# Three-product scores for three batches, 48-row paced loads, and warming products only at the start, in a recurrence-plus-attention kernel

## The chip, the cores and the metric

One core of a Trainium2 chip runs the whole program in one launch. The metric is device time in microseconds (us) of one execution; lower is better. Engines are named as in the profile: PE (TensorE products), PEld (its weight loads), DVE (VectorE), ACT (ScalarE), POOL (GpSimd), SP (the engine that issues the DMAs here).

## What is computed

A gated linear recurrence over 768 steps (4 batches, 8 heads of 48 channels), then four causal attention experts over its output, of which each row takes its best two. In the input, wq and wk are scaled by about 29, so that the scores are large.

```python
for t in range(S):                                  # S = 768, D = 48
    cur = np.einsum('bhd,bhe->bhde', u[None] * kt, vt)
    y[:, :, t] = np.einsum('bhd,bhde->bhe', rt, state + cur)
    state = wt[:, :, :, None] * state + np.einsum('bhd,bhe->bhde', kt, vt)
...
for e in range(E):                                  # E = 4, D = 384, Hd = 64
    q = x @ wq[e]; k = x @ wk[e]; v = x @ wv[e]
    scores = scale * (q @ k.transpose(0, 2, 1))
    scores = np.where(causal, -1000000000.0, scores)
    a = np.exp(scores - scores.max(-1, keepdims=True))
    a /= a.sum(-1, keepdims=True) + 1e-09
    ye = a @ v @ wo[e]
    # added to the rows whose best two experts include e, times the gate
```

## The kernel before, in words

The work is cut into eight units, one for each batch b and half g of the sequence (384 rows). A unit has two parts. The recurrence (`rwkv`, from line 316 on) works on four pairs of heads p: SP loads the streams of decay, key and receptance (tile `lt`, 128 partitions of 1166 numbers, each head padded from 48 to 64 partitions), the same data in row order (`nat`) and the values (`vy`). DVE and POOL form decay products and running products (`w2`, `suf`, `pre`, `kt`, with `kw` and `rw` written in place into `lt`), PE transposes the keys (`ktp`), forms state updates (`ups`), in-chunk scores (`aps`) and outputs (`yps`), DVE carries the state from chunk to chunk (`wst`, line 406). The attention (`moe`, from line 623 on) works for two pairs of experts ep: projections `proj` (line 665; product of high and low parts, three products each in the format fp32r for every unit but the first), evacuation of Q and K from PSUM (`qd`, lines 674 to 680), values (`vproj`), scores (`sc`, line 761), maximum on DVE (line 771), exponential on ACT (line 776), transposes of the weights (`tp`), product with the values (`av`, line 818) and the output projection (`op`, line 886).

A score tile takes 128 rows of Q against 128 to 768 columns of K, with the two experts of a pair in the upper and lower 64 rows of PE's array. Q and K are float32 there:

```python
for h in range(np_):
    o = slice(h * w, (h + 1) * w)
    for x in range(2):
        p = slice(64 * x, 64 * x + 64)
        nc.tensor.matmul(spv(x)[:, h, :], q()[p, t], flat(k())[p, o], start=True, stop=True)
```

PE transposes 128x128 blocks in one of two ways (`turn`, lines 217 to 224): whole (line 220) where the product ahead of it uses the whole array, and as two 64-row halves side by side (line 224) where the array is already split.

The order of all instructions is written out by hand in the string `ORDER` (line 975 on): a letter for the engine and the number of the planned operation. `Plan.order` (line 125) walks through it, gives out buffers and emits. Each engine executes its own instructions in that order; across engines only data, buffers and semaphores bind. SP's loads wait only for their buffer (four `lt`, three `nat`, three `vy`) and for a free DMA semaphore. `warm` (line 938) are products on zeros with no reader; 33 of the 94 planned stand in the order, all in the early part.

Of the kernel before, what the change touches and what calls it, by code (L numbers as in the profile page):

```python
# [27 lines left out]
WB = NH * (C2 + 1) + 1  # L28

# [6 lines left out]
def t_scan(cols):  # L36
    return 95 + 2.09 * cols
# [10 lines left out]
def t_pool(cols):  # L48
    return {144: 415, 192: 550, 199: 580, 240: 655, 288: 785, 384: 905}[cols]
# [142 lines left out]
def rwkv_moe(ctx: ExitStack, tc: tile.TileContext, wkr, vY, nat, uN, uT,  # L192
# [9 lines left out]
    def sb(shape, dt, tag, name):  # L202
        return Slot(wk, shape, dt, tag, name)

# [111 lines left out]
    def rwkv(b, g, v0, v1):  # L316
# [54 lines left out]
        def keys(group, n):  # L371
# [25 lines left out]
            for x, (p, kt, kts, vn, na, suf, sfv, ys) in enumerate(group):  # L397
                want(p / (NP + 1))
                ws, kw = wst[p], ("wst", p)
                for c in range(NH - g):  # L400
                    i, a = divmod(c, 2)

                    def grow(e, c=c, o=columns(x, a, i), ws=ws, sfv=sfv):
                        new = ws[0:112, c0 + c, :]
                        if c0 + c:
                            nc.vector.scalar_tensor_tensor(new, ws[0:112, c0 + c - 1, :], sfv()[0:112, c, 0:1], upk()[0:112, o], op0=ALU.mult, op1=ALU.add)  # L406
                        else:
                            copy(e, new, upk()[0:112, o])
                    if c0 + c:
                        plan.add("ws", {"DVE": 172}, grow, [upk, suf, kw + (c0 + c - 1,)], [kw + (c0 + c,)])  # L410
                    else:
                        plan.add("us", {"ACT": 200, "DVE": 115}, grow, [upk], [kw + (0,)])
# [5 lines left out]
                plan.add("ys", {"DVE": t_dve((NH - 1 + g) * D), "POOL": t_pool((NH - 1 + g) * D)}, scaled, [suf] + [kw + (c0 - g + c,) for c in range(NH - 1 + g)], [ys])  # L418
# [3 lines left out]
        for p in range(NP):  # L422
            n = f"{b}{g}{p}"
            want(p / (NP + 1))
            lt = sb([128, 2 * WB + 2 * NH * C], F32, "lt", f"lt{n}")
            if first and p == 0:
                load("ld", lambda lt=lt: lt()[:, 0:2 * WB], wkr[b, g, p, :, 0:2 * WB], 2 * WB, [(lt, 0)])
                load("ld", lambda lt=lt: lt()[:, 2 * WB:], wkr[b, g, p, :, 2 * WB:], 2 * NH * C, [(lt, 1)])
            else:
                load("ld", lt, wkr[b, g, p], 2 * WB + 2 * NH * C, [(lt, 0), (lt, 1)])  # L430
# [53 lines left out]
            if first:  # L484
# [13 lines left out]
                plan.add("rkm", {"PE": 360}, sums, [(na, 1), "ut"], [rkb], mode="Q")  # L498
# [5 lines left out]
                plan.add("rk", {"DVE": 145, "ACT": 390}, kept, [rkb], [rk])  # L504
# [22 lines left out]
            if not first:  # L527
# [12 lines left out]
                plan.add("rk", {"DVE": t_dve(288), "ACT": 1250}, rks, [(na, 2)], [rk, (na, 2)])  # L540
# [9 lines left out]
            plan.add("ux", dict(prod(288), ACT=1370), ux, [vy if first else (na, 0), rk], [(xn, p)])  # L550
# [72 lines left out]
    def moe(b, g, v0, v1):  # L623
# [7 lines left out]
        if g == 0:  # L631
            BT["K"] = [sb([128, 2, 384], F32, f"K{ep}", f"K{b}{ep}") for ep in range(2)]
            BT["v"] = [sb([128, NT, 128], F32, f"v_sb{ep}", f"v_sb{b}{ep}") for ep in range(2)]
        K, v_sb = BT["K"], BT["v"]
        Q = [sb([128, 384], F32, f"Q{ep}", f"Q{n0}{ep}") for ep in range(2)]
# [11 lines left out]
        def proj(ep, qk):  # L647
# [4 lines left out]
            for k in range(3):  # L652
# [10 lines left out]
                def mm(e, k=k):  # L663
                    for j, (w, x) in enumerate(((wqh, xh), (wql, xh), (wqh, xl))):
# [3 lines left out]
                         claim=[(K if qk else Q)[ep]])  # L668
            if qk == 0:
# [35 lines left out]
        def gates():  # L705
# [15 lines left out]
            plan.add("gate", {"DVE": 365}, compare, lgk, [m1, c1, c2])  # L721
# [7 lines left out]
            plan.add("gate", {"POOL": 1440}, ranks, lgk + ["masks", m1], [c1, c2, rank, ge])  # L729
            plan.add("gate", {"ACT": 250}, lambda e: nc.scalar.activation(ge(), ge(), AF.Exp), [ge], [ge])  # L730
# [7 lines left out]
            plan.add("gate", {"POOL": 875}, norm, [ge, c1], [gs, c1])  # L738

        def scores(ep, i):  # L740
# [8 lines left out]
            q, k = Q[ep], K[ep]  # L749

# [11 lines left out]
            plan.add("sc", {"PE": T_SC[3 * g + i]}, mm, [q] + [(k, gg) for gg in range(g + 1)],  # L762
# [63 lines left out]
        def gather(i0, i1):  # L826
# [12 lines left out]
            plan.add("g3", {"DVE": 610}, over, [(asum, i, x) for i in range(i0, i1) for x in range(E)] + [ge, gs], [gg])  # L839
# [91 lines left out]
    plan.add("masks2", {"DVE": 1400}, masks2, [], ["masks"])  # L931
# [19 lines left out]
    held = None  # L951
    for o in plan.order(dict(PE=7200.0 - 216 * WARM[0], DVE=3000.0, ACT=1700.0, POOL=3000.0, SP=1800.0)):
# [5 lines left out]
        e = o["e"]  # L958
        if e in BOTH and o["kind"] in BOTH[e]:
# [13 lines left out]
BUFS.update(K0=2, K1=2, Q0=2, Q1=2)  # L973
# [3 lines left out]
P29 P30 P31 P32 P33 P126 V139 A127 V143 P34 P140 S113 P128 V146 A141 V144 V147 P15 S171 S138 A129 V148 P8 P11 S235 V145 P151 V176 A152 P18 V149 P10  # L977
P153 V177 P161 P25 S236 S196 V173 A125 S172 V198 S250 V130 G180 V178 V131 P6 V162 G205 A154 P12 P28 V132 V164 G182 S4 V133 P35 P174 V155 V134 G135
V179 P185 A175 P14 V201 A186 V206 A150 V202 S99 P187 P166 V238 V188 V156 G207 V189 V157 A0 V190 V158 V191 G181 A167 V159 V192 A184 S197 P36 P210 V203
V193 G160 P199 V183 V204 G194 S289 P168 V239 A211 A200 V208 P212 V246 A169 S251 V242 A213 P37 P229 V253 P220 V214 A230 G243 V240 V215 A209 V216 S104  # L980
V247 V241 V217 S304 G245 V221 A248 V223 P1127 P1131 G219 V244 P225 A249 V257 S107 V254 V258 P227 V259 S252 A226 V255 V218 A100 S290 V261 V296 P231
A228 V292 P265 V256 A232 P233 S291 V293 P1128 A234 S352 A266 V307 V260 P1129 A267 V294 V297 P268 V101 A1130 A105 P281 S305 V308 V262 P1074 V300 A263
A264 P1075 S367 V295 P1076 V301 P1066 V312 V299 P1067 V106 S237 V298 A1077 P1070 P1071 A284 A1078 V311 S408 V360 P1072 V313 V275 G315 V282 A1073 A302
V276 P1132 P1068 S368 V309 V269 G285 V277 V270 P319 V1079 V271 V278 V272 G359 P1086 V279 A320 V273 P1087 V310 G280 A321 P1133 V370 V355 G274 V314 P322
V356 S423 P335 A1069 A303 V371 P286 V329 A338 G375 G316 V330 V323 V324 V331 G378 A1134 V325 V332 P1088 A102 V326 S306 V357 V287 P19 S353 V333 A317 P26
V327 G374 P1080 V288 P1081 V103 G334 P1097 A318 P1106 G328 V415 V358 P1082 V1107 G339 V1109 A1108 V1098 V336 P1115 A1084 A1090 A1110 G361 V1100 P1111
V1091 V1085 V372 P340 A1112 V373 A1101 A1099 V1116 G416 V1118 A1117 G377 P1104 V341 P1113 A1105 V342 A1114 P1120 V376 A1119 P1102 P346 V362 S488 A1103
A1121 V411 P1122 A347 V1092 P400 A1123 V412 A1083 A1089 V348 P349 G379 S409 V403 A350 P343 P1124 G430 A344 A380 S369 S473 G1093 V401 P1125 P1126 V345
# [149 lines left out]
```

## Time and profile before

| | us |
|---|---|
| device time, median of 3 runs | 338.61 |
| lowest and highest run | 336.25, 338.82 |
| profiled execution, span from first to last instruction | 335.0 |
| PE busy, DVE busy, ACT busy, POOL busy | 315.5, 267.8, 237.6, 142.2 |
| DMA: bytes moved, mean rate | 44.13 MB, 132 GB/s |

For the profiled execution only the span is given, no device time of its own; the median of the runs is 3.6 us above that span and the lowest run 1.3 us. The busy times add up what each engine executes, with PE's ends modelled. A chain of waits is followed back from the last instruction; "issue" in it is time in which an engine waited for nothing that the profile shows.

### The profile page before, as it was taken

To read this page: it belongs to the slowest core of one execution; us is meant where nothing else is said; L and a number is where in the kernel's file an instruction comes from. 1 tells how busy PE (TensorE), PEld (TensorE's weight loads), DVE (VectorE), ACT (ScalarE), POOL (GpSimd) and SP (SyncE) were. 2 spreads that over 40 slices of the span, in tenths; PEclk is the share of its full clock that TensorE was granted. 3 is DMA by queue.
4 is the path that set the end of the run, shared out by engine and by line. 5 is a ranking of instruction groups with operands and counts; after the bars stand their busy time and mean duration, and the time that the engine had idled before them with its cause. 6 is when DMAs were issued, how large, how long until landed. Compare 5 with 4: busy or idle time off the path is not lost.

```text
span 335.0 us, 12951 instructions
## 1 busy us (share of the span) xinstructions
PE 315.5 (94%) x5174; PEld 246.3 (74%) x5174; DVE 267.8 (80%) x863; ACT 237.6 (71%) x842; POOL 142.2 (42%) x275
## 2 busy tenths in 40 slices
PE   8969988999999997969999999999999999999995
PEld 3647666777866975869777758789778867877684
DVE  6978989999999897957979887999765565675752
ACT  2358888998899774936787968758856484548861
POOL 2341166478565567532666646573600000310230
PEclk9998999999999999998999999999999999999999
DMA  7997760654625486372563092532000001001021
GB/s 259 323 285 269 235 214 34 232 179 129 223 102 215 143 268 210 97 251 72 157 202 108 4 346 73 155 90 70 4 0 26 0 3 48 3 25 70 2 72 70
DMA packets 18204, 44.13 MB, mean 132 GB/s; under 512 B 2144, under 2 KB 10080, under 8 KB 18144
## 3 DMA queue, kind: packets, MB, share of 16 engines
q1 hardware_dynamic: 18144, 43.30, 38.7%
q8 instruction: 41, 0.67, 0.8%
q14 instruction: 19, 0.16, 0.1%
HBM read 38.58 MB, written 4.72 MB: 129 GB/s over the span
## 4 chain that ended last, share of the span: by engine, by line
PE 82%; DVE 10%; issue 5%; ACT 2%; POOL 0%; POOLq 0%
PE pp L665 13%; PE yp L818 12%; PE sp L761 10%; PE op L886 7%; PE vp L697 6%; PE tp L224 4%; PE aps L572 4%; PE tp L220 4%; PE yps L350 3%; PE ups L395 3%; PE yps L348 3%; PE pp L658 2%; PE warm L938 2%; DVE wst L406 2%; DVE a L771 2%
## 5 line engine op out<-in xcount | busy, mean ns | idle before, releaser
L776 ACT ACTIVATE a<-a,mx 128x256 f32<-128x256 f32 (+5 forms) x96 | 64.2, 670 | 10.2 <-DVE mx L771 8.6
L771 DVE CUSTOM_DVE_ANT_0 a<-sp,causal 128x384 f32<-128x384 f32 (+5 forms) x96 | 56.4, 616 | 15.0 <-PE sp L761 8.8
L228 ACT COPY ATa<-tp 128x512 f32<-128x512 f32 (+3 forms) x73 | 35.2, 490 | 24.1 <-PE tp L224 12.2
L761 PE MATMUL sp<-K,Q 64*128 64x384 f32 (+4 forms) x256 | 45.9, 470 | 0.5 <-DVE mx L771 0.4
L406 DVE SCALAR_TENSOR_TENSOR wst<-wst,suf,ups 112x48 f32<-112x48 f32 x160 | 35.9, 256 | 3.8 <-ACT wst L228 2.9
L818 PE MATMUL yp<-ATa,v_sb 128*64 128x384 f32 (+2 forms) x240 | 36.3, 430 | 0.2 <-DVE ge L731 0.2
L546 ACT ACTIVATE xn<-nat,rk 128x48 f32<-128x48 f32 x132 | 32.2, 331 | 0.7 <-DVE rk L539 0.7
L665 PE MATMUL pp<-xh,wh_qk 128*128 128x384 f32 x84 | 31.6, 376 | 0.0
L350 PE MATMUL yps<-ys,pre 64*64 64x48 f32 (+1 forms) x704 | 25.4, 220 | 6.4 <-issue 6.4
L761 PEld LDWEIGHTS sp<-K,Q 64*128 64x128 f32 x256 | 21.6, 187 | 10.7 <-issue 4.5
L350 PEld LDWEIGHTS yps<-ys,pre 64*64 64x64 f32 (+1 forms) x704 | 22.3, 134 | 9.1 <-issue 8.3
L665 PE MATMUL pp<-xh,wl_qk 128*128 128x384 f32 x84 | 29.0, 345 | 0.0
L665 PE MATMUL pp<-xl,wh_qk 128*128 128x384 f32 x84 | 28.9, 344 | 0.0
L224 PEld LDWEIGHTS tp<-ident,a 64*128 64x128 f32 x442 | 19.2, 138 | 12.9 <-ACT ATa L228 4.0
L416 POOL TENSOR_TENSOR ys<-wst,suf 112x240 f32<-112x240 f32 (+1 forms) x32 | 25.4, 805 | 4.1 <-DVE wst L406 2.3
L348 PE MATMUL yps<-vy,am 64*64 64x48 f32 x768 | 25.9, 220 | 0.4 <-issue 0.4
L818 PEld LDWEIGHTS yp<-ATa,v_sb 128*64 128x64 f32 x240 | 15.3, 136 | 14.5 <-issue 9.2
L224 PE MATMUL tp<-ident,a 64*128 64x64 f32 x442 | 23.1, 228 | 2.1 <-issue 1.3
L348 PEld LDWEIGHTS yps<-vy,am 64*64 64x64 f32 x768 | 23.1, 134 | 0.0
L697 PE MATMUL vp<-wh_vg,xh 128*128 128x260 f32 x63 | 19.7, 313 | 2.6 <-issue 2.6
L537 ACT ACTIVATE nat<-nat 128x48 f32<-128x48 f32 x90 | 20.6, 236 | 0.9 <-ACT ATa L228 0.5
L518 POOL TENSOR_TENSOR kt<-lt,suf 128x384 f32<-128x384 f32 x19 | 17.8, 936 | 6.5 <-DVE suf L507 1.9
(152 smaller groups left out, 859.7 us busy)
## 6 DMA issues: line engine op xcount, KB each, us to landing
lt<-in_wkr_dram SPq DMA_DIRECT2D x31, 583.0 KB, 5.3
nat<-in_nat_dram SPq DMA_DIRECT2D x28, 432.0 KB, 4.0
vy<-in_vY_dram SPq DMA_DIRECT2D x32, 144.0 KB, 3.8
out_dram<-ob SPq DMA_DIRECT2D x24, 192.0 KB, 2.0
w_qk<-in_wqk_dram SPq DMA_DIRECT2D x1, 768.0 KB, 6.9
nat<-in_nat_dram SPq DMA_DIRECT2D x4, 144.0 KB, 5.9
w_vg<-in_wvg_dram SPq DMA_DIRECT2D x1, 390.0 KB, 6.6
lt<-in_wkr_dram SPq DMA_DIRECT2D x1, 384.0 KB, 3.2
```

Source lines behind the costliest of these rows:

```text
L224: nc.tensor.transpose(o()[:, h * 512 + i * 64:h * 512 + i * 64 + 64], src[r], ident[r, r])
L228: nc.scalar.copy(o, i)
L348: nc.tensor.matmul(to, am()[k, c, :], vy()[k, c, :], start=zero and x == 0, stop=not first and i == 2 and x == len(group) - 1)
L350: nc.tensor.matmul(to, pre()[r, c, 0:C], ys()[r, c, :], start=i == x == 0, stop=False)
L406: nc.vector.scalar_tensor_tensor(new, ws[0:112, c0 + c - 1, :], sfv()[0:112, c, 0:1], upk()[0:112, o], op0=ALU.mult, op1=ALU.add)
L546: nc.scalar.mul(xn()[:, i, (2 * p + h) * D:(2 * p + h + 1) * D], v()[:, i, h, :], rk()[:, i, h:h + 1])
L665: nc.tensor.matmul(pp()[:, 0:384], w[:, qk, k, cs], x()[:, k, :], start=(k == j == 0), stop=(k == j == 2))
L697: nc.tensor.matmul(vp()[:, 0:260], x()[:, k, o], w[:, k, :], start=(k == j == 0), stop=(k == j == 2))
L761: nc.tensor.matmul(spv(x)[:, h, :], q()[p, t], flat(k())[p, o], start=True, stop=True)
L771: nc.vector.tensor_tensor_reduce(out=a()[:, 0:n].rearrange("p (a n) -> p a n", a=np_), in0=spv(x), in1=causal[:, S - n:S].rearrange("p (a ...
L776: plan.add("exp", {"ACT": t_exp(n)}, lambda e, x=x, y=y, mx=mx, a=a: nc.scalar.activation(a()[:, 0:n], a()[:, 0:n], AF.Exp, bias=mx(), sca ...
L818: nc.tensor.matmul(yp()[e * 64:e * 64 + 64, lo:hi], v_sb[ep]()[:, j, e * 64:e * 64 + 64], at, start=(j == 0), stop=(j == nj - 1))
```

## The change

For batches 1, 2 and 3 (`SPLIT`) Q and K are stored in fp32r (the high part), and a second tile each (`Ql`, `Kl`) takes what is left of the projection in PSUM after the high part is subtracted (kind `ql`, DVE). A score is then three fp32r products that add up in PSUM: Q with K, Ql with K, Q with Kl. Batch 0 keeps its float32 scores. The loads of `lt` for all units but the first are two DMAs of 48 rows each into four kept tiles whose padding rows stay from the first unit's loads. Every SP instruction waits in addition for the last PE instruction that stands ahead of it in the order ("pace"). Of the warming products 14 are left instead of 33. The order is written anew as a whole, with it the split of some operations between DVE, ACT and POOL, and some costs in the plan. The scratch space for DMA descriptors is set to 2048 bytes.

```diff
-            lt = sb([128, 2 * WB + 2 * NH * C], F32, "lt", f"lt{n}")
+            lt = streams(f"lt{n}")
...
+                def rows(e, lt=lt, p=p):
+                    for h in range(2):
+                        nc.sync.dma_start(lt()[64 * h:64 * h + D, :], wkr[2 * b + g - 1, p, h])
+                plan.add("ld", {"SP": 1300}, rows, w=[(lt, 0), (lt, 1)])
...
+                if b in SPLIT:
+                    plan.add("ql", {"DVE": t_dve(384)}, lambda e: nc.vector.scalar_tensor_tensor(
+                        Ql[ep](), pp()[:, 0:384], 0.125, h().bitcast(F32), op0=ALU.mult, op1=ALU.subtract), [pk, h], [Ql[ep]])
...
+                if b in SPLIT:
+                    plan.add("ql", {"DVE": t_dve(384)}, lambda e: nc.vector.tensor_tensor(
+                        Kl[ep]()[:, g, :], pp()[:, 0:384], h()[:, g, :].bitcast(F32), op=ALU.subtract), [pk, (h, g)], [(Kl[ep], g)])
...
+            terms = [(q, k), (Ql[ep], k), (q, Kl[ep])] if split else [(q, k)]
...
-                    for x in range(2):
-                        p = slice(64 * x, 64 * x + 64)
-                        nc.tensor.matmul(spv(x)[:, h, :], q()[p, t], flat(k())[p, o], start=True, stop=True)
+                    for j, (q_, k_) in enumerate(terms):
+                        for x in range(2):
+                            p = slice(64 * x, 64 * x + 64)
+                            nc.tensor.matmul(spv(x)[:, h, :], q_()[p, t], flat(k_())[p, o], start=j == 0, stop=j == len(terms) - 1)
...
+        if e == "PE":
+            pe = [x for x in nc.cur_bb.bb.instructions[n:] if x.engine == nc.tensor.engine][-1]
+        elif e == "SP" and pe is not None:
+            own = next(x for x in nc.cur_bb.bb.instructions[n:] if x.engine == nc.sync.engine)
+            tc.add_manual_dep(own, pe.name, mybir.DependencyInfo(mybir.DependencyClass.Sync, mybir.DependencyReason.DATA), reason="pace")
...
-S110 S111 V2 S3 S136 P17 V1 P9 P13 P5 P7 P16 V117 P22 S112 V118 S170 V119 V114 V120 P20 P21 P23 P24 P27 P115 V122 S137 A116 V121 V124 S195 V123 V142
+S110 S111 V1 S3 V2 V117 V118 S136 V119 V114 V120 S113 V121 V122 S195 V123 V142 S138 V139 V124 S112 V147 P21 S170
...
+SPLIT = (1, 2, 3)
```

PE, the last score tile of batch 1, second half, first pair of experts (`sp` scores, `pp` projections of the next unit, `xp` and `tp` transposes). Before:

```order
L665 MATMUL pp2011_3699<-xl20_3341,wh_qk_99 128x384
L761 MATMUL sp11020_3741<-K10_2694,Q110_3011 128x384
L761 MATMUL sp11021_3743<-K10_2694,Q110_3011 128x384
L761 MATMUL sp11020_3741<-K10_2694,Q110_3011 128x384
L761 MATMUL sp11021_3743<-K10_2694,Q110_3011 128x384
L224 MATMUL xp210_3758<-ident_77,xn21_3022 128x64 x6
```

And now:

```order
L787 MATMUL sp11020_3794<-K10_2547,Q110_3049 128x384
L787 MATMUL sp11021_3796<-K10_2547,Q110_3049 128x384
L787 MATMUL sp11020_3794<-K10_2547,Ql110_3051 128x384
L787 MATMUL sp11021_3796<-K10_2547,Ql110_3051 128x384
L787 MATMUL sp11020_3794<-Kl10_2617,Q110_3049 128x384
L787 MATMUL sp11021_3796<-Kl10_2617,Q110_3049 128x384
...
L232 MATMUL tp1031_3822<-ident_81,a1031_3486 128x64 x4
```

Four float32 products became twelve fp32r products (the second six, for the other half of the columns, repeat the first), and a transpose of the weights stands behind them in place of one of the next unit's input.

DVE, where Q of that tile is taken out of PSUM (`Ql` the low part, `suf`, `w2`, `pre` the recurrence of a later unit, `lg` the gate's logits). Now:

```order
L726 COPY lg11_3035<-vp112_3001 128x4
L522 RECIPROCAL inv_pre_75<-suf211_2764 128x6
L696 SCALAR_TENSOR_TENSOR Ql110_3051<-pp1100_3039,Q110_3049 128x384
L520 SCALAR_TENSOR_TENSOR suf212_3053<-w2212_3014,one_suf_72 128x198
L520 SCALAR_TENSOR_TENSOR suf213_3055<-w2213_2891,one_suf_72 128x198
L524 SCALAR_TENSOR_TENSOR w2211_2674<-w2211_2674,inv_pre_75 128x198
```

The row with `Ql` has no counterpart before, where ACT alone took this Q out of PSUM; the recurrence of the later unit now queues behind it.

SP, the first loads of the program (`lt` streams, `vy` values, `nat` row order, `w_qk` weights). Before:

```order
L237 DMA vy001_240<-in_vY_dram 128x288
L237 DMA lt010_249<-in_wkr_dram 128x1166
L237 DMA nat010_308<-in_nat_dram 128x864
L237 DMA nat003_310<-in_nat_dram 128x288
L237 DMA vy002_320<-in_vY_dram 128x288
L237 DMA lt011_323<-in_wkr_dram 128x1166
L933 DMA u_sb_86<-in_uN_dram 128x384
L237 DMA w_qk_391<-in_wqk_dram 128x1536
L237 DMA vy003_455<-in_vY_dram 128x288
```

And now:

```order
L245 DMA nat001_139<-in_nat_dram 128x288
L442 DMA lt0_66<-in_wkr_dram 48x1166 x2
L245 DMA nat003_157<-in_nat_dram 128x288
L960 DMA u_sb_90<-in_uN_dram 128x384
L245 DMA w_qk_198<-in_wqk_dram 128x1536
L442 DMA lt1_67<-in_wkr_dram 48x1166 x2
L245 DMA vy003_250<-in_vY_dram 128x288
L245 DMA nat002_268<-in_nat_dram 128x288
L245 DMA nat010_346<-in_nat_dram 128x864
```

The second unit's first streams come as two DMAs of 48 rows, and its large row-order load (`nat010`) moved behind the last small loads of the first unit.

## Rows read from the trace of the kernel before

**Rows 1.** The page's head and its busy times.
```profile
span 335.0 us, 12951 instructions
PE 315.5 (94%) x5174; PEld 246.3 (74%) x5174; DVE 267.8 (80%) x863; ACT 237.6 (71%) x842; POOL 142.2 (42%) x275
```
**Rows 2.** Stretches: length; PE, PEld, DVE, ACT, POOL busy (instructions), clock, DMA share, GB/s.
```profile
50.00:100.00 50.00, 47.54 (x878) 36.96 (x878) 48.72 (x161) 44.90 (x183) 32.89 (x54) 1.00 0.44 152
100.00:240.00 140.00, 132.70 (x2608) 108.74 (x2606) 120.55 (x400) 103.74 (x375) 80.38 (x141) 0.99 0.46 147
240.00:335.00 95.00, 91.42 (x823) 70.57 (x815) 56.59 (x174) 58.31 (x158) 12.29 (x48) 1.00 0.08 28
```
**Rows 3.** Timeline of PE, 170 to 179 us: start, duration, operation, count.
```profile
171.21 0.34 PE L665 MATMUL pp<-xh,wl_qk 128*128 128x384 f32 x1
...
172.44 0.34 PE L665 MATMUL pp<-xl,wh_qk 128*128 128x384 f32 x1
...
174.22 0.43 PE L224 MATMUL tp<-ident,a 64*128 64x64 f32 x6
174.57 0.44 PE L665 MATMUL pp<-xh,wh_qk 128*128 128x384 f32 x1
...
177.52 1.56 PE L761 MATMUL sp<-K,Q 64*128 64x384 f32 x8
178.91 0.35 PE L224 MATMUL xp<-ident,xn 64*128 64x64 f32 x6
```
**Rows 4.** DVE's group that subtracts a high part from PSUM.
```profile
L611 DVE TENSOR_TENSOR xl<-xp,xh 128x384 fp32r<-128x384 f32 x21 | 11.1, 549 | 0.6 <-ACT xh L609 0.6
```
**Rows 5.** Chain of waits, a run of each kind of transpose: start, length.
```profile
113.01 1.53 PE tp L220 x14
...
273.95 1.60 PE tp L224 x42
```
**Rows 6.** Chain of waits, stretches in which PE waits for nothing shown.
```profile
21.29 2.60 issue
...
47.74 0.81 issue
...
108.41 0.79 issue
...
119.09 0.64 issue
...
131.69 2.22 issue
...
146.62 2.56 issue
...
192.66 0.68 issue
```
**Rows 7.** Stretches between those waits, columns as in rows 2.
```profile
21.29:47.74 26.45, 23.48 (x505) 17.50 (x506) 22.86 (x70) 18.94 (x82) 7.12 (x10) 0.94 0.73 245
...
119.09:131.69 12.60, 11.96 (x253) 9.32 (x252) 11.52 (x34) 7.37 (x22) 8.61 (x14) 1.00 0.90 305
```
**Rows 8.** DMA queues of the page, the one for instructions.
```profile
q8 instruction: 41, 0.67, 0.8%
```
**Rows 9.** Stretches with a lower clock, columns as in rows 2.
```profile
25.00:30.00 5.00, 5.00 (x80) 3.55 (x72) 3.22 (x10) 3.85 (x22) 1.48 (x2) 0.77 0.97 362
...
150.00:155.00 5.00, 5.00 (x24) 4.97 (x24) 3.74 (x14) 2.40 (x9) 0.00 (x0) 0.66 0.03 7
```
**Rows 10.** The group of the warming products.
```profile
L938 PE MATMUL warm<-causal 128*128 128x512 bf16 x33 | 11.7, 479 | 1.5 <-POOL causal L247 1.4
```
**Rows 11.** DMA issues of the streams, KB each, median us to landing.
```profile
lt<-in_wkr_dram SPq DMA_DIRECT2D x31, 583.0 KB, 5.3
```
**Rows 12.** Timeline of PE, two products of 260 columns, as rows 3.
```profile
295.93 0.28 PE L697 MATMUL vp<-wl_vg,xh 128*128 128x260 f32 x1
296.05 0.28 PE L697 MATMUL vp<-wh_vg,xl 128*128 128x260 f32 x1
```

More of the change, by code (lines that the diff above doesn't have):

```diff
@@ L28 @@
 WB = NH * (C2 + 1) + 1
+LT = 2 * WB + 2 * NH * C
 def t_dve(cols):
@@ L203, in sb, with streams @@
         return Slot(wk, shape, dt, tag, name)
+    kept_ = [cst.tile([128, LT], F32, name=f"lt{i}") for i in range(BUFS["lt"])]
+    def streams(name):
+        s = sb([128, LT], F32, "lt", name)
+        s.make = lambda i: kept_[i]
+        return s
     def bank(tag, name, dt=F32, whole=True):
@@ L411, in keys @@
                     else:
-                        plan.add("us", {"ACT": 200, "DVE": 115}, grow, [upk], [kw + (0,)])
+                        plan.add("us", {"ACT": 110, "DVE": 115}, grow, [upk], [kw + (0,)])
                 def scaled(e, ys=ys, ws=ws, sfv=sfv):
@@ L417, in scaled @@
                                         sfv()[0:112, o, 0:1].to_broadcast([112, NH - 1 + g, D]), op=ALU.mult)
-                plan.add("ys", {"DVE": t_dve((NH - 1 + g) * D), "POOL": t_pool((NH - 1 + g) * D)}, scaled, [suf] + [kw + (c0 - g + c,) for c in range(NH - 1 + g)], [ys])
+                plan.add("ys", {"DVE": t_dve((NH - 1 + g) * D), "POOL": 680 if g == 0 else 645}, scaled, [suf] + [kw + (c0 - g + c,) for c in range(NH - 1 + g)], [ys])
         group = []
@@ L503, in kept @@
                         copy(e, rk().rearrange("p i h -> p (i h)")[k], rkb()[k, h * 512:h * 512 + NH])
-                plan.add("rk", {"DVE": 145, "ACT": 390}, kept, [rkb], [rk])
+                plan.add("rk", {"DVE": 145, "ACT": 240}, kept, [rkb], [rk])
             plan.add("w2", prod(WB), lambda e, w2=w2, w_=w_: E_[e].tensor_tensor(w2(), w_(0), w_(1), op=ALU.mult),
@@ L549, in ux @@
                                         op=ALU.mult)
-            plan.add("ux", dict(prod(288), ACT=1370), ux, [vy if first else (na, 0), rk], [(xn, p)])
+            plan.add("ux", dict({"DVE": t_dve(288), "POOL": 650}, ACT=1360), ux, [vy if first else (na, 0), rk], [(xn, p)])
             kts = sb([128, 3, 128], F32, "kts", f"kts{n}")
@@ L720, in compare @@
                 nc.vector.tensor_tensor(c2(), la, lb, op=ALU.is_equal)
-            plan.add("gate", {"DVE": 365}, compare, lgk, [m1, c1, c2])
+            plan.add("gate", {"DVE": 310}, compare, lgk, [m1, c1, c2])
             def ranks(e):
@@ L737, in norm @@
                 V.tensor_scalar(gs(), gs(), 1e-9, None, op0=ALU.add)
-            plan.add("gate", {"POOL": 875}, norm, [ge, c1], [gs, c1])
+            plan.add("gate", {"POOL": 760}, norm, [ge, c1], [gs, c1])
         def scores(ep, i):
@@ L749, in scores @@
             q, k = Q[ep], K[ep]
+            split = b in SPLIT
+            terms = [(q, k), (Ql[ep], k), (q, Kl[ep])] if split else [(q, k)]
             def spv(x):
@@ L838, in over @@
                 nc.vector.tensor_tensor(gg()[:, t], gg()[:, t], ge()[:, t], op=ALU.mult)
-            plan.add("g3", {"DVE": 610}, over, [(asum, i, x) for i in range(i0, i1) for x in range(E)] + [ge, gs], [gg])
+            plan.add("g3", {"DVE": 550}, over, [(asum, i, x) for i in range(i0, i1) for x in range(E)] + [ge, gs], [gg])
             def parts(e):
@@ L930, in rwkv_moe @@
     plan.add("masks3", {"DVE": 200}, masks3, [], ["dmask"])
-    plan.add("masks2", {"DVE": 1400}, masks2, [], ["masks"])
+    plan.add("masks2", {"DVE": 1880}, masks2, [], ["masks"])
     plan.add("ldut", {"SP": 475}, lambda e: nc.sync.dma_start(u_t, uT), [], ["ut"])
```

208 lines of the change are left out of this document (113 added, 95 removed).

## The prediction

> **What bounds the kernel now.** I read the page's busy times first. PE is busy for 94% of the span of 335.0 us, DVE for 80%, ACT for 71% [rows 1]. These are averages, so the table of stretches comes next. From 50 to 100 us both PE (47.5 of 50) and DVE (48.7 of 50) are full; from 100 to 240 us PE is busy for 132.7 of 140 us and DVE for 120.6, or 86%; from 240 us on, when the recurrence is over, DVE needs only 56.6 of 95 us, and PE 91.4 [rows 2]. So PE sets the pace nearly everywhere, DVE beside it in the second stretch. A busy PE is still not a PE that makes progress, so I looked in the chain of waits for the places where it stands still. Seven pieces there are called "issue", time for which no other engine is the reason: 2.60, 0.81, 0.79, 0.64, 2.22, 2.56 and 0.68 us, together 10.3 us [rows 6].
>
> What are they? Between the first and the second of them PE executes 505 products, between the fourth and the fifth (119.09 and 131.69 us) 253 [rows 7]. The whole kernel has 5174 products and as many weight loads [rows 1], and the queue that fetches instructions moves 41 packets with 0.67 MB [rows 8], which is 126.2 products with their loads for each packet. 505 / 126.2 = 4.00 and 253 / 126.2 = 2.00: PE stops at the ends of fetched blocks. It waits for its own instructions, which come through the same DMA engines as the data (0.90 of their time is taken in the stretch before 131.69 us, rows 7). [...]
>
> [...]
>
> **The sum, made against the span of 335.0 us.** The median of the runs is 3.6 us above it, and I add these 3.6 at the end.
>
> 1. Scores. A score tile of 768 columns starts at 177.52 us, and what follows it starts at 178.91 us: 1.39 us, or 1.81 ns a column, in float32 with two experts side by side. The projections' fp32r products of 384 columns start at 171.21 us and, seven products later, at 172.44, a step of 0.176 us [rows 3], so three products cost 3 x 0.176 / 384 = 1.37 ns a column if the two experts still run side by side. That saves 0.44 ns a column. A batch and a pair of experts has tiles of 128 to 768 columns, 2688 in all; two pairs and three batches make 16128 columns and 36 tiles, 7.1 us. If part of a tile's time doesn't depend on its columns, up to the 0.12 us that term 2 finds for a change of the array's split, it stays, and 36 x 0.12 = 4.3 us less go. Bounds -7.1 and -2.8; I take -5.0, the middle. All of it is PE's time and none is hidden in the last stretch.
>
> 2. Transposes and changes of the array's split. By the order, 92 of 187 whole transposes become pairs of halves, since a split product now stands ahead of them. A whole one takes 1.53 / 14 = 0.109 us, a pair 1.60 / 21 = 0.076 us [rows 5]: 92 x 0.033 = -3.0 us. But the order changes between split and whole array 176 times instead of 153. Three pairs take 0.35 us from 174.22 to 174.57 [rows 3], 0.12 more than 3 x 0.076, and I put that down to such a change: 23 x 0.12 = +2.8. Bounds -3.0 and +2.8, taken -0.2.
>
> 3. The start. Nineteen warming products go, 11.7 / 33 = 0.35 us each [rows 10], 6.7 us of PE at most; most of it lay in PE's waits for DVE, whose own instructions don't change much there. [...] Fewer bytes help (see 6). Bounds -6.7 and +12.5, taken -1.0, as PE is not the only engine that is late there.
>
> 4. Instruction fetch. The count of PE's instructions grows: scores from 128 float32 products with four records each to 32 of these and 288 with two, +192; transposes +184; warming -38: +338, one more block in 41. The streams, each 583.0 KB that land in 5.3 us [rows 11], carry 48 of 64 rows, 437 KB, in 28 of 32 cases; 4.1 of 44 MB go. The pace keeps SP from sending a burst whenever a buffer comes free, yet nothing in the order says that no burst meets the end of a block. Bounds: all 13.2 us go, or the stalls grow by half, +5. I take -4.0, somewhat above the quarter by which the streams shrink.
>
> 5. DVE. Twenty-four subtractions from PSUM come in, 0.549 us each as for the input's low part [rows 4]: 13.2 us. By the order 13 of them (7.1 us) stand ahead of the last state step, but the number of DVE rows up to there falls from 635 to 632, so 16 others have left that part, at a mean of 267.8 / 863 = 0.31 us [rows 1] some 5 us. In the last part there is room (38 of 95 us idle, rows 2). Queued behind a subtraction are the recurrence's scans of a later unit, and scores wait for it one instruction longer than for Q alone. Bounds 0 and +7.1; taken +1.0, hidden by PE's work but for a few places.
>
> 6. The queue of SP. Loads that were one issue are two, and each waits for the PE instruction ahead of it; behind a waiting load stand all later loads and the output's stores. If a stream is sent only when it is needed, DVE and POOL wait for it: 0 to +5.3 us, one landing [rows 11], at the start, where nothing covers it. Later four tiles cover it. Taken +1.0.
>
> Sum: -5.0 - 0.2 - 1.0 - 4.0 + 1.0 + 1.0 = -8.2, a span of 326.8 us and a time of 330.4.
>
> **Rivals.** A measurement tells about 1% (3.4 us) from no change.
>
> *Swallowed.* The stalls move with the new order and stay as long (0 in place of -4.0), and DVE takes half of its bound (+3.5 for +1.0): 330.4 + 4.0 + 2.5 = 336.9, no change. For it: nothing in the order looks at block ends, and DVE is at 97% from 50 to 100 us [rows 2]. Against it: 10% fewer bytes, and fewer DVE rows before the last state step. Chance 0.20.
>
> [...] Chance 0.11.
>
> *Weight loads don't overlap.* Each of the three products needs weights of 128 columns for its half of the array. If the load comes before its product instead of beside an earlier one, a load costs up to the 0.12 us of a product of 260 columns that has one of its own [rows 12]; 24 product pairs for the six tiles make 24 x 0.12 us + 2688 x 1.37 ns = 6.6 us against 2688 x 1.81 ns = 4.9 before, six times: +10.2 for -5.0 gives 345.6, slower. Against it: products of 384 and 260 columns with new weights each follow at 0.176 and 0.12 us, the same 0.46 ns a column [rows 3, 12], in the whole array. Chance 0.05. [...]
>
> *All stalls go.* With the streams smaller and paced no fetch waits any more, and the clock never falls: -13.2 for -4.0 gives 321.2. For it: both large stalls in the middle came in or after stretches of heavy transfer [rows 7]. Against it: one block more, no change to the other loads. Chance 0.14.
>
> **How the numbers follow.** The forecast has 0.50, with a range of its own from 326 to 335. Faster by over 1% (below 335.2): 0.47 of it, all of the last rival and 0.02 of the first, 0.63. Slower (above 342.0): the two slow rivals but 0.01, 0.15. The rest, 0.22, is within 1%. The range from 321 to 342 leaves out most of the slow rivals and a little of the fast one, under 0.2.
>
> **What would show it.** Right: the group of scores falls by 5 us or so in time from its starts, with 768 columns in some 1.15 us; the chain's "issue" pieces add up to 6 us or less; DVE's subtractions stay near 0.55 us and DVE below 90% from 100 to 240 us. Wrong: score products of 384 columns at a step well above 0.18 us; a granted clock near 0.5 up to 30 us; stalls of PE of over 2 us after a pair of streams was sent; DVE or POOL waiting for `lt`. If the stalls stay and the time falls all the same, term 1 or 3 was too small.

## The result and the profile after

The changed kernel takes 326.75 us (median of four runs, 325.29 to 329.57), the kernel before 338.54 beside it (336.25 to 338.82): the ratio is 0.9736, with a 95% interval from 0.9686 to 0.9786, or 8.9 us less. (The two medians alone differ by 11.8 us, a ratio of 0.965; beside the later experiments the kernel before has medians of 336.3 to 337.3, so the smaller figure is the safer one, and all that follows is in ratios.) The forecast was 330.4, in a range from 321 to 342. Below, "us by ratio" is a difference of two ratios times 337 us; from the two intervals it is certain to about 2.5 us, in the widest case 2.8. The profiled run of the changed kernel is its slowest, 329.57 us with a span of 327.8, so the traces below tell where time goes, and the ratios how much.

The page's head [rows 1 for before]:

```profile
span 327.8 us, 13409 instructions
PE 311.1 (95%) x5343; PEld 253.0 (77%) x5343; DVE 275.6 (84%) x876; ACT 237.0 (72%) x860; POOL 144.3 (44%) x277
```

PE is busy for 4.4 us less though it executes 169 products more; DVE is busy for 7.8 us more. The stretches [rows 2], columns: length; PE, PEld, DVE, ACT, POOL busy with instructions; granted clock; DMA share; GB/s:

```profile
50.00:100.00 50.00, 48.53 (x935) 38.91 (x927) 49.03 (x160) 44.85 (x179) 30.70 (x55) 1.00 0.61 161
100.00:230.00 130.00, 125.20 (x2589) 104.53 (x2587) 118.90 (x385) 98.09 (x377) 78.78 (x133) 0.99 0.49 132
230.00:327.80 97.80, 94.19 (x1006) 77.60 (x1004) 63.80 (x198) 64.04 (x182) 14.58 (x54) 1.00 0.09 33
```

DVE fills 91% of the middle stretch (86% before). From 50 to 100 us the DMA engines are busy for 0.61 of the time at 161 GB/s, where it was 0.44 at 152: a busier set of engines that moves hardly more. Hold on to that.

A score tile of 768 columns on PE's timeline [rows 3] (start, length, operation, count):

```profile
294.75 0.34 PE L682 MATMUL pp<-xl,wh_qk 128*128 128x384 f32 x1
295.02 0.45 PE L787 MATMUL sp<-K,Q 64*128 64x384 f32 x2
295.30 0.34 PE L787 MATMUL sp<-K,Ql 64*128 64x384 f32 x2
295.48 0.34 PE L787 MATMUL sp<-Kl,Q 64*128 64x384 f32 x2
295.65 0.34 PE L787 MATMUL sp<-K,Q 64*128 64x384 f32 x2
...
296.18 0.41 PE L232 MATMUL tp<-ident,a 64*128 64x64 f32 x8
```

From 295.02 to 296.18 it takes 1.16 us (1.39 before). The first pair of products, one for each expert, takes 0.28 us; from then on each follows the last after 0.175 us, just as the projections do: the two experts run side by side and no weight load shows. DVE's subtractions [rows 4]:

```profile
L696 DVE SCALAR_TENSOR_TENSOR Ql<-pp,Q 128x384 fp32r<-128x384 f32 x12 | 6.6, 547 | 0.4 <-ACT Q L691 0.4
L702 DVE TENSOR_TENSOR Kl<-pp,K 128x384 fp32r<-128x384 f32 x12 | 6.5, 549 | 1.4 <-ACT K L236 1.4
```

The table of PE's waits holds what answers to rows 6 (engine, operation, waited for: us in total, times, longest):

```profile
PE yps L358 <- issue: 1.7, 1, 1.7
PE pp L682 <- DVE Ql L696: 1.0, 1, 1.0
PE yp L845 <- DVE Ql L696: 0.4, 1, 0.4
PE aps L585 <- issue: 0.4, 1, 0.4
```

One stall of 1.7 us and one of 0.4 remain, 2.1 us; before, the same table gives 11.1, of which 10.3 are the seven pieces of rows 6 (the chain before has an eighth, of 0.58 us at 87.29 us, that isn't PE's). New are waits for `Ql`: by the code the next projection needs the PSUM bank that the subtraction still reads. (The chain of waits also has "issue" pieces at 9.44, 83.69 and 95.41 us, where other engines wait; the expectations below that speak of 3.3 us count the last two with the 1.7. From here on I count by PE's table alone.) The clock [rows 9], columns as in rows 2:

```profile
20.00:25.00 5.00, 5.00 (x150) 5.00 (x151) 5.00 (x14) 2.16 (x9) 0.49 (x1) 0.50 0.78 217
25.00:30.00 5.00, 4.74 (x88) 3.94 (x84) 3.42 (x15) 3.41 (x13) 1.87 (x2) 0.50 1.03 234
...
160.00:165.00 5.00, 3.31 (x73) 2.10 (x65) 3.19 (x15) 1.93 (x9) 2.67 (x5) 0.82 0.05 14
165.00:170.00 5.00, 5.00 (x55) 4.13 (x52) 3.28 (x11) 2.58 (x7) 1.18 (x4) 0.84 0.00 0
```

The 1.7 us stall is followed by 1.7 us of lost clock (0.18 x 5 + 0.16 x 5), so fetching costs 3.4 us. Before it cost somewhat more than the 13.2 of the forecast (10.3 us of stalls by rows 6 and 0.23 x 5 + 0.34 x 5 = 2.9 us of clock by rows 9), which left out that the lower clock after the first stall begins before 25 us:

```profile
20.00:25.00 5.00, 2.40 (x91) 2.28 (x95) 3.25 (x7) 1.20 (x6) 1.57 (x3) 0.88 0.91 311
```

That is 0.12 x 5 = 0.6 us more, 3.5 us of clock and 13.8 us in all. In the changed kernel the granted clock is 0.50 from 20 to 30 us at the start as well, which is 5 us of full clock.

### The profile page after: what moved, and what is told of

The parts are those of the page before. It is cut to its first block, busy times and chain, and to the rows that moved or that the text cites. A ratio compares the mean times of both kernels' runs of the same rounds, so it can differ in the third digit from the quotient of the medians.

```text
span 327.8 us, 13409 instructions
## 1 busy us (share of the span) xinstructions
PE 311.1 (95%) x5343; PEld 253.0 (77%) x5343; DVE 275.6 (84%) x876; ACT 237.0 (72%) x860; POOL 144.3 (44%) x277
## 3 DMA queue, kind: packets, MB, share of 16 engines
q1 hardware_dynamic: 17696, 39.13, 43.5%
## 4 chain that ended last, share of the span: by engine, by line
PE 64%; DVE 21%; issue 6%; ACT 4%; DMA 3%; POOL 1%; SPq 1%; DVEq 0%; POOLq 0%; ACTq 0%
PE yp L845 10%; PE sp L787 9%; PE pp L682 9%; PE op L913 7%; PE vp L720 6%; PE tp L232 5%; PE ups L403 3%; PE yps L358 3%; DVE wst L414 3%; DVE a L798 3%; PE yps L356 2%; PE aps L585 2%; DVE w L524 2%; DMA lt<-in_wkr_dram 2%; DVE am L590 2%
## 5 line engine op out<-in xcount | busy, mean ns | idle before, releaser
L798 DVE CUSTOM_DVE_ANT_0 a<-sp,causal 128x128 f32<-128x128 f32 (+5 forms) x96 | 56.7, 618 | 19.3 <-PE sp L787 14.4
L803 ACT ACTIVATE a<-a,mx 128x128 f32<-128x128 f32 (+5 forms) x96 | 64.2, 670 | 8.9 <-DVE mx L798 8.9
L787 PE MATMUL sp<-K,Q 64*128 64x384 f32 (+4 forms) x160 | 31.0, 423 | 1.1 <-DVE xl L624 0.6
L559 ACT ACTIVATE xn<-nat,rk 128x48 f32<-128x48 f32 x120 | 29.0, 327 | 1.3 <-DVE rk L552 1.3
L232 PEld LDWEIGHTS tp<-ident,a 64*128 64x128 f32 x530 | 22.0, 139 | 7.0 <-issue 1.6
L232 PE MATMUL tp<-ident,a 64*128 64x64 f32 x530 | 26.0, 228 | 0.7 <-ACT ATa L236 0.4
L533 POOL TENSOR_TENSOR pre<-lt,w 128x384 f32<-128x384 f32 x18 | 16.8, 936 | 17.6 <-DVE lt L529 5.6
L424 POOL TENSOR_TENSOR ys<-wst,suf 112x240 f32<-112x240 f32 (+1 forms) x28 | 21.7, 787 | 2.9 <-DVE wst L414 2.0
L787 PEld LDWEIGHTS sp<-K,Q 64*128 64x128 f32 x160 | 15.3, 188 | 8.4 <-issue 3.2
L902 POOL TENSOR_TENSOR yl<-yr,yh 128x384 fp32r<-128x384 f32 x9 | 9.0, 1009 | 26.8 <-ACT yh L901 26.7
## 6 DMA issues: line engine op xcount, KB each, us to landing
lt<-in_wkr_dram SPq DMA_DIRECT2D x56, 218.6 KB, 4.1
```

Source lines behind the costliest of these rows:

```text
L232: nc.tensor.transpose(o()[:, h * 512 + i * 64:h * 512 + i * 64 + 64], src[r], ident[r, r])
L559: nc.scalar.mul(xn()[:, i, (2 * p + h) * D:(2 * p + h + 1) * D], v()[:, i, h, :], rk()[:, i, h:h + 1])
L787: nc.tensor.matmul(spv(x)[:, h, :], q_()[p, t], flat(k_())[p, o], start=j == 0, stop=j == len(terms) - 1)
L798: nc.vector.tensor_tensor_reduce(out=a()[:, 0:n].rearrange("p (a n) -> p a n", a=np_), in0=spv(x), in1=causal[:, S - n:S].rearrange("p (a ...
L803: plan.add("exp", {"ACT": t_exp(n)}, lambda e, x=x, y=y, mx=mx, a=a: nc.scalar.activation(a()[:, 0:n], a()[:, 0:n], AF.Exp, bias=mx(), sca ...
```

## Experiments

**The pace.** In the changed kernel without SP's waits for PE:

```diff
-        elif e == "SP" and pe is not None:
...
-            tc.add_manual_dep(own, pe.name, ..., reason="pace")
```

> The changed kernel with SP's waits for PE (the pace) left out, all else the same. Theory A (pace and fewer bytes keep bursts of loads off the fetch of PE's instructions; the chain's issue pieces went from 10.3 to 3.3 us): stalls come back, issue pieces of 6 to 10 us, time 330 to 334 against 326.8. Rival B (the new order and the smaller streams did that, the pace is idle): issue pieces of 2 to 5 us and 325.5 to 328.

0.9734 [0.9687, 0.9782], 328.0 us: no difference. Its waits:

```profile
PE aps L585 <- issue: 2.2, 1, 2.2
PE yps L356 <- issue: 1.1, 1, 1.1
...
PE ups L403 <- issue: 0.8, 1, 0.8
```

4.1 us in place of 2.1, at other places, and the same time: B holds, what took the stalls away is not the pace.

**The scores.** One float32 product again, without and with the subtractions (in the second nobody reads the low parts):

```diff
-            terms = [(q, k), (Ql[ep], k), (q, Kl[ep])] if split else [(q, k)]
+            terms = [(q, k)]
```

> The changed kernel with float32 scores in one product for all batches and without the 24 subtractions, same order otherwise. Theory A (the scores are PE's time and nothing hides it): 768 columns in 1.39 us again, +5 to +7 us of PE less what the 24 subtractions cost on DVE (up to 1): 330.5 to 333.5. Rival B (what the scores save is eaten by the subtractions or hidden by DVE): 326 to 328.5.

> The changed kernel with float32 scores in one product, as in the run without subtractions (0.984), but with the 24 subtractions left in, their results read by nobody. PE's instructions are the same in both, so the difference is what the subtractions cost on DVE, and the difference to the changed kernel (0.974) what the three products save on PE. Theory A (DVE's part is the 1 us of the forecast): 0.984 to 0.988. Rival B (DVE bounds enough of the middle that half of their 13 us shows): 0.992 to 1.005. Rival C (wholly hidden): 0.981 to 0.984.

Without: 0.9837 [0.9803, 0.9872]; with: 0.9864 [0.9809, 0.9918]. Both have the same instructions on PE, so the subtractions cost +0.9 us by ratio (not told from 0; B's 0.992 lies just outside the interval). From the second to the changed kernel the three products save 4.3 us. A holds in the first; in the second A's range has the measured ratio, but C's (wholly hidden) lies in the interval too.

**The streams.** Whole streams of 128 rows in one DMA; then two DMAs of 64 rows; then two DMAs of all 128 rows, each with half of the columns. The last two move the same bytes as the first:

```diff
-                        nc.sync.dma_start(lt()[64 * h:64 * h + D, :], wkr[2 * b + g - 1, p, h])
+                    nc.sync.dma_start(lt(), wkr[2 * b + g - 1, p])
...
+                        nc.sync.dma_start(lt()[64 * h:64 * h + 64, :], wkr[2 * b + g - 1, p, h])
...
+                        o = slice(h * LT // 2, (h + 1) * LT // 2)
+                        nc.sync.dma_start(lt()[:, o], wkr[2 * b + g - 1, p, :, o])
```

> The changed kernel with streams of 128 rows in one DMA, as before (4.1 MB more), paced as now. Theory A (bytes count in the fetch of instructions and in the first 30 us, where the DMA engines are full): issue pieces 1 to 4 us longer and the first state steps 1 to 2 us later, 328 to 331. Rival B (the pace or the order alone does it): 326 to 327.8.

> The changed kernel with its streams still as two DMAs, but of 64 rows each, padding rows included. The 48-row pieces held the 16 DMA engines for 0.37 us a row by the page's shares, whole streams for 0.22 us. Theory A (48 rows are what the engines share out badly): 0.21 to 0.26 us a row, DMA share some 41%, ratio 0.961 to 0.967. Rival B (two DMAs on half of the partitions each are what costs): 0.33 us or more a row, DMA share over 45%, ratio 0.972 to 0.980.

> The changed kernel with each stream of 128 rows as two DMAs of 128 partitions and half of the columns. Two DMAs of 64 rows held the DMA engines for 47.7% of the span and gave 0.984, one DMA of 128 rows 40.8% and 0.963. Theory A (two DMAs for one are what costs): share 46% or more, ratio 0.978 to 0.988. Rival B (DMAs that reach only half of the partitions are what costs): share 40 to 43%, ratio 0.960 to 0.968.

Whole: 0.9627 [0.9577, 0.9676]. Both theories of the first run fall: the 4.1 MB that come back make the kernel 3.7 us faster. Two of 64 rows: 0.9841 [0.9777, 0.9905], a little above B's range; two by columns: 0.9608 [0.9542, 0.9674]. The DMA view has the queue of the loads (packets, MB, share of 16 engines) and the streams' issues (count, KB each, median us to landing). The changed kernel:

```profile
q1 hardware_dynamic: 17696, 39.13, 43.5%
...
lt<-in_wkr_dram SPq DMA_DIRECT2D x56, 218.6 KB, 4.1
```

Whole streams:

```profile
q1 hardware_dynamic: 18144, 43.30, 40.8%
...
lt<-in_wkr_dram SPq DMA_DIRECT2D x31, 583.0 KB, 4.4
```

Two DMAs of 64 rows:

```profile
q1 hardware_dynamic: 18592, 43.31, 47.7%
...
lt<-in_wkr_dram SPq DMA_DIRECT2D x56, 291.5 KB, 4.8
```

Two DMAs by columns:

```profile
q1 hardware_dynamic: 22176, 43.31, 42.3%
...
lt<-in_wkr_dram SPq DMA_DIRECT2D x56, 291.5 KB, 3.8
```

Shares times span times 16 engines: whole streams hold the engines for 0.408 x 321.0 x 16 = 2095 us, two of 64 for 0.477 x 329.9 x 16 = 2518 us with the same bytes. That is 423 us more for 28 streams. By columns it is 0.423 x 321.5 x 16 = 2176 us, with 4000 more and smaller packets. The traces also time every packet: one row of 4664 bytes takes 0.220 us on average with whole streams, 0.299 with two DMAs of 64 rows and 0.298 in the changed kernel with 48. (The 0.37 and 0.22 us a row in the second expectation are worked out with all other bytes at the whole streams' mean rate.) So 48 rows run no worse than 64, and it isn't two DMAs for one that costs, but DMAs that write to only half of the partitions: theory A of the 64-row run, that 48 rows are badly shared out, falls, and so does A of the columns. One thing changes together with the partitions, the rows in one DMA; 64 rows spread over all partitions weren't run.

The place where it hurts is the start. The stretch from 10 to 20 us with whole streams:

```profile
10.00:15.00 5.00, 4.91 (x91) 3.35 (x91) 5.00 (x17) 3.04 (x15) 0.34 (x1) 1.00 1.02 343
15.00:20.00 5.00, 4.29 (x126) 3.36 (x124) 5.00 (x16) 2.35 (x9) 3.89 (x6) 1.00 0.91 320
```

And in the changed kernel:

```profile
10.00:15.00 5.00, 4.52 (x64) 2.73 (x66) 3.90 (x11) 2.63 (x13) 0.00 (x0) 1.00 0.96 243
15.00:20.00 5.00, 4.23 (x83) 3.38 (x85) 4.97 (x20) 1.87 (x7) 3.75 (x6) 0.99 1.03 254
```

Both have the DMA engines full or nearly so, but one gets 320 to 343 GB/s out of them and the other 243 to 254. DVE's first state update (`wst`) starts at 14.5 us with whole streams and at 16.1 in the changed kernel, the 17th 2.9 us later than with whole streams; up to the 113th the gap stays between 1.6 and 3.3 us. The rest of the 6.8 us between these two profiled spans comes only after that, with the stall at 160.5 us and the lower clock behind it, so these traces give the streams some 3 us, near the 3.7 of the ratios.

**The warming products.** The 19 back in the changed kernel, and 19 left out of the kernel before (both by the string of the order: `+P..` and `-P..`, 19 times).

> The changed kernel with 33 warming products in place of 14, the 19 others ahead of the same PE work as before the change. [...] Rival B (the clock lost at the start counts): 321 to 325. Rival C (warming products stand in PE's way): 329 to 333.

> The kernel before with 14 of its 33 warming products (the first five and every second of the others). Theory A (the first 30 us wait for loads and DVE): ratio 0.995 to 1.005. Rival B (warming products stand in PE's way): 0.980 to 0.992. Rival C (the clock is lost without them): 1.008 to 1.03, with a granted clock near 0.5 for over 10 us.

0.9751 [0.9707, 0.9796] and 0.9998 [0.9945, 1.0051]: neither can be told from the kernel that it starts from. In the changed kernel with 33 products the clock is full where it was 0.50 (it is 0.68 from 10 to 15 us, where the changed kernel has 1.00), and the time is the same:

```profile
20.00:25.00 5.00, 4.25 (x169) 3.56 (x167) 5.00 (x13) 3.25 (x10) 1.07 (x2) 1.00 0.82 217
25.00:30.00 5.00, 4.92 (x88) 3.23 (x84) 4.61 (x19) 2.68 (x11) 1.36 (x2) 1.00 1.03 251
```

Seven of DVE's state updates run from 46.2 to 47.7 us in both traces, that with 33 products and the changed kernel's: PE's clock is not what the first 30 us wait for. The first run, 328.12 us and by ratio 0.5 us above the changed kernel, lies between the ranges of B and C; in the second A holds. The second run is no test of the clock, which is full there (1.00 on average up to 23.37 us) with 14 products as well. And both runs move the ends of the fetched blocks by 19 products, which counts by itself, as the shifts below show: with 14 products the kernel before has 3.6 us less of stalls (7.5 for 11.1) and loses 3.4 us more by its clock (0.979 on average in the profiled execution, 0.989 with 33).

**The order alone.** Float32 scores, no subtractions, whole streams, no pace, 33 warming products: all the edits above together, in the changed kernel's order. (The four kept tiles and the scratch space of 2048 bytes stay too.)

> The changed kernel with everything taken back but its order (and which engine takes which operation): float32 scores, no subtractions, whole streams, no pace, 33 warming products. Theory A (the parts add up as the runs so far say: scores +0.010, whole streams -0.011, pace and warming products about 0): ratio to the kernel before 0.970 to 0.979, so that the order is the main part of the gain. Rival B (the order gains only together with the other parts): 0.985 to 1.000.

0.9723 [0.9660, 0.9787], 9.3 us by ratio: A, the order is the main part. PE's waits in it:

```profile
PE aps L584 <- issue: 1.8, 2, 1.3
...
PE yps L356 <- issue: 1.1, 1, 1.1
PE yps L358 <- issue: 1.0, 1, 1.0
...
PE ups L403 <- issue: 0.4, 1, 0.4
```

And its page's row of the granted clock, in 40 slices of the span:

```profile
PEclk9999999999999999999999999999999999999999
```

4.3 us of stalls for 11.1, and a clock that is nowhere below nine tenths (3.5 us were lost before): 10.3 us, more than the gain of 9.3. By this account nothing of it is left for shorter work. The stalls are from one profiled execution of each; the clock is not: on average it is 0.998 in the four runs of this kernel and 0.987 in the 13 of the kernel before beside it, some 4 us of the span.

**Where the blocks end.** The kernel before with each warming product cut into three of a third of its columns, and the changed kernel with each cut into four: no more work, but 66 and 42 products more ahead of all that follows.

```diff
-    lambda e, w=w: nc.tensor.matmul(w()[:, 0:512], wz[:, 0:128], wz, start=True, stop=True)
+    lambda e, w=w: [nc.tensor.matmul(w()[:, a:b], wz[:, 0:128], wz[:, a:b], start=True, stop=True)
+                    for a, b in ((0, 172), (172, 344), (344, 512))]
```

> The kernel before, each of the 33 warming products cut into three of a third of its columns: no more work, but 66 products with their loads more at the start, so that every later end of a fetched block comes 66 products (about half a block, some 3 us) earlier in the work. Theory A (a stall is a block's end that meets a burst of loads, by chance): the stalls of 2.22 and 2.56 us at 131.7 and 146.6 us move to other work and change in length, issue pieces sum to 3 to 7 us in place of 10.3, ratio 0.980 to 0.992. Rival B (every stretch of heavy loads costs its stall wherever the ends lie): sum 9 to 12 us, ratio 0.996 to 1.004. Rival C (the stalls belong to the work, not to block ends): the same two products wait again.

> The changed kernel with each of its 14 warming products cut into four, 42 products more at the start and no more work, so that the ends of fetched blocks come a third of a block earlier in the work. Theory A (how many ends meet a burst of loads is chance, in this order as in the old one): stalls at the same counts of products, but in other work and of other lengths; issue pieces of PE sum to 2 to 8 us (3.3 without the shift), ratio 0.965 to 0.990. Rival B (the new order with its pace keeps ends and bursts apart): sum at most 3.5 us, ratio 0.970 to 0.977.

0.9869 [0.9808, 0.9931] and 0.9815 [0.9751, 0.9879]. The first is 4.4 us faster than the kernel before with no work taken away (stalls 8.5 us for 11.1); the second is 2.7 us slower than the changed kernel, but the intervals overlap, so that this difference is not certain (stalls 6.7 us for 2.1). Where do they stop? Stretches from 0 to the start of a stall count the products executed (the first x). The kernel before:

```profile
0.00:21.29 21.29, 18.93 (x347) 11.52 (x347) 17.89 (x57) 9.45 (x36) 8.09 (x21) 1.00 0.85 288
0.00:108.41 108.41, 99.82 (x1988) 72.82 (x1989) 98.69 (x313) 83.37 (x334) 53.91 (x96) 0.98 0.61 208
0.00:119.09 119.09, 109.71 (x2241) 82.16 (x2242) 108.20 (x344) 92.32 (x367) 60.19 (x108) 0.99 0.60 201
```

The kernel before, shifted:

```profile
0.00:19.92 19.92, 17.00 (x347) 15.21 (x348) 16.41 (x56) 8.18 (x31) 7.33 (x21) 1.00 0.89 294
0.00:108.72 108.72, 99.98 (x1988) 78.20 (x1989) 97.79 (x310) 82.60 (x329) 54.62 (x95) 0.97 0.62 208
0.00:119.20 119.20, 109.53 (x2242) 87.28 (x2243) 107.05 (x339) 91.30 (x359) 60.01 (x103) 0.97 0.60 200
```

The changed kernel:

```profile
0.00:160.50 160.50, 149.67 (x3003) 119.55 (x3004) 150.87 (x484) 123.09 (x499) 89.98 (x156) 0.97 0.68 181
```

The changed kernel, shifted:

```profile
0.00:22.70 22.70, 16.82 (x348) 14.93 (x348) 18.64 (x56) 9.09 (x31) 6.46 (x19) 1.00 0.88 258
...
0.00:95.03 95.03, 82.97 (x1738) 66.39 (x1739) 86.83 (x278) 69.12 (x286) 46.59 (x85) 0.98 0.74 196
0.00:109.72 109.72, 97.04 (x1991) 77.15 (x1992) 99.78 (x316) 81.74 (x320) 55.00 (x97) 0.98 0.69 181
0.00:120.70 120.70, 106.83 (x2244) 85.42 (x2245) 109.61 (x345) 90.38 (x357) 60.72 (x111) 0.99 0.68 181
```

347, 1988 and 2241 products in the kernel before, 347, 1988 and 2242 in the shifted one, though up to 66 of them are now others: the stall sits at a count, not at a piece of work, and rival C falls. In the last, 1738, 1991 and 2244 are 253 apart, two blocks of 126.5, and the 3003 of the changed kernel are 21 blocks behind 347. Of the two long stalls of the kernel before, of 2.22 and 2.56 us, the shifted one has 0.33 us of the first left and nothing of the second, and new ones of up to 1.6 us stand at other ends. Its sum lies between what A and B expected; its time is A's. In the changed kernel A holds, and B falls by its stalls (6.7 us where it allowed 3.5).

All fourteen traces together show more. They have 60 stalls of PE of 0.3 us or more, and 57 of them stand within four products of a block's end. The queue for instructions has one packet for each end (41 before [rows 8], 42 in the changed kernel), and the traces time these packets. At each of the 57 stalls PE goes on 2.2 to 3.0 us after the start of its packet, with the DMA engines busy or idle; at the 511 ends without such a stall PE gets there 2.2 us or more after that start. So a stall is what is left of that time when PE is through with its block too early: of 46 blocks that PE ran through in under 3.5 us 34 ended in a stall, of 210 that took over 8 us none did. The kernel before has six such short blocks and stalls behind each; the order alone has five, the changed kernel one, the changed kernel shifted three. A burst of loads goes with a later start of the packet: in the median 2.3 us behind the last end where the DMA engines were over 0.9 busy in the 3 us ahead of it, 0.5 us where they were under 0.1. But a stall doesn't need one. In the kernel before with 14 warming products, PE stands still for 1.84 us at 59.70 us, after 977 products (five blocks behind 347), and the 3 us ahead of it are almost free of loads:

```profile
56.70:59.70 3.00, 2.66 (x95) 1.94 (x95) 2.96 (x17) 2.81 (x12) 2.19 (x4) 1.00 0.02 5
```

This is read from the traces; no run put long or short products at an end on purpose.

**A version that beats both.** Whole streams and no pace.

> The changed kernel with whole streams in one DMA each and without the pace: the two parts that the runs so far show as a loss and as idle, both taken back. Theory A (they add up): ratio 0.959 to 0.967, issue pieces of 2 to 5 us. Rival B (with whole streams the pace does keep stalls away): 0.968 to 0.978, issue pieces of 5 us or more.

322.35 us, 0.9570 [0.9516, 0.9624]: A, a little better than its range. It lies 1.7% below the changed kernel; from whole streams with the pace (0.9627) it isn't told apart.

## Why the prediction was right, and where only its number was

The time was 3.7 us too high and well in the range (by ratio the change was -8.9 where -8.2 was said), but two of the six steps were wrong, with errors that partly cancel: that the sum came so near is in part luck.

1. *Scores, -5.0.* Right in mechanism and size: 1.16 us for 768 columns where 1.15 was said, and 4.3 us by ratio. The rival of weight loads that don't overlap falls by the step of 0.175 us.

2. *Transposes and splits, -0.2.* Not run by itself. The order alone gives 9.3 us, and its stalls and clock account for 10.3, so no effect of its size shows; that it is right isn't shown either.

3. *The start, -1.0.* The two runs on the warming products give 0 within 2.5 us. No run shows the +12.5 us of the upper bound, or a slow start that costs time (chance 0.11): the granted clock is 0.50 from 20 to 30 us, 5 us of full clock, and with 1.00 there, in the run with 33 products, the time stays. Not PE sets that stretch; DVE, full from 20 to 25 us (5.00 of 5), and the loads, with the DMA engines full from 25 to 30 (1.03), are what is left.

4. *Instruction fetch, -4.0: the step that failed by size.* By the traces it went from 13.8 us (13.2 in the forecast, from rows 6 and 9) to 3.4, -10.4, some three quarters of what "All stalls go" took. The reasons given, smaller streams and the pace, were wrong: without pace, and with whole streams, stalls stay at 1.2 to 4.3 us. What did it is the new order, which puts other work at the block ends. "Swallowed" had the right thought, that nothing in the order looks at block ends, but the draw came out well. The argument should have been: six of the eight stalls at block ends come where PE runs through a block in under 3.5 us, a new order cuts the blocks anew, and a kernel with a bad draw is likelier to improve. Most ends of blocks show no stall: of some 40, two do in the changed kernel, 2.1 us in all, and eight did before, 10.7 us.

5. *DVE, +1.0.* Measured +0.9 (0 is within its error), with subtractions of 0.547 and 0.549 us for the 0.549 of the forecast, and PE waiting 1.4 us for them. DVE is at 91% from 100 to 230 us, a little over the 90% named as a sign; it cost no more.

6. *SP's queue and the pace, +1.0: the step that failed in kind.* The pace costs nothing that is measured. What costs is the shape of the loads: 3.7 us by ratio, at the start, where this step expected its loss, and inside the upper bound of 5.3, but that bound was worked out for a late issue. The sign that the forecast named, POOL or DVE waiting for `lt`, is there in the changed kernel's table of waits:

```profile
POOL lt L529 <- DMA lt<-in_wkr_dram: 1.9, 3, 1.3
```

All such waits add up to 4.3 us there, to 2.6 with whole streams, to 9.4 with two DMAs of 64 rows and to none in the kernel before, so part of them comes with the new order.

I took 10% fewer bytes as a help in steps 3, 4 and the rivals; the rows of before show streams of 128 rows only, and the forecast set no bound for how a DMA on part of the partitions runs.

Added up: order with its stalls -9.3, scores -4.3, subtractions +0.9, streams +3.7, pace and warming products about 0, is -9.0, and -8.9 is measured. Each of these terms is certain to some 2.5 us only, so that the sum closes to 0.1 is chance.

What stays open: how far the order's gain would survive other block ends. Two shifts moved the time by -4.4 and, less certainly, +2.7 us, as much as the scores or the streams are worth; and every run above that adds or takes away products, those on the scores and on the warming products too, moved the ends as well. An order that keeps PE from running through a block in under 3.5 us wasn't tried.

## What to carry to other kernels

Before crediting a new order with a gain, shift the ends of the fetched blocks with products that cost nothing: if the time moves by 1% (here by -4.4 us, and less certainly by +2.7), that much of any comparison is where the ends fell. Look first for runs of short products that fill a whole block: they are where PE waited for its instructions here (34 of the 46 blocks that it ran through in under 3.5 us ended in a stall). Judge a load by its DMA share and GB/s, not by its bytes: here, cutting padding rows out of a load made the engines slower by more than the bytes were worth (43.5% of their time for 39.13 MB, where whole streams took 40.8% for 43.30). And when a forecast comes true, take the parts back one at a time all the same; here the largest part and the only loss were both not where the forecast had them.

## What the hardware showed that was not expected

A DMA of 48 rows of 4.7 KB (218.6 KB) took 4.1 us from issue to landing in the median, about as long as one of 128 such rows (583 KB, 4.4 us), and two of 64 rows held the engines for 20% longer than one of 128 rows with the same bytes (2518 against 2095 us), where two of half columns took 4% longer.

PE stopped at the same counts of executed products, 347, 1988 and 2241 or 2242, whichever work stood there, and went on 2.2 to 3.0 us after the start of the packet with its next instructions. And a clock of 0.50 over 10 us at the start cost no time that could be measured, while the stalls of 2.60 and 2.56 us before [rows 6, 9] and of 1.7 us after were each followed by a lower clock that lost another 1.7 us (0.12 x 5 + 0.23 x 5, 0.34 x 5, and 0.18 x 5 + 0.16 x 5).
